# Decode attention over two caches on one core: PV in four column groups, V in one slot, 64 KB rows, B's heads in groups of eight

## The chip, the cores and the metric

The kernel runs on one core of a Trainium2 chip. A core has TensorE (PE: matrix multiplications into PSUM), VectorE (DVE), ScalarE (ACT), GpSimd (POOL) and SyncE (SP), each with its own in-order queue of instructions, and 16 DMA engines that move data between HBM and the on-chip memory SBUF (128 partitions). PE has a clock that a throttle grants in part. The metric is device microseconds from launch to end of the one core, the median of several runs.

## The reference

Two attention layers, A and B, each for one query token of 32 heads with 128 channels. A attends over all 16384 cached keys of each head, B over the last 4096. Then each multiplies by its output matrix, and the two rows of 512 are put side by side.

```python
def _A_ref(x, k_cache, v_cache, wq, wo):          # x [1,1,512], caches [1,32,16384,128] bf16
    q = ((x @ wq).reshape(B, Sq, 32, 128)).transpose(0, 2, 1, 3)
    scores = jnp.einsum("bhqd,bhkd->bhqk", q, k_cache) * (128 ** -0.5)
    p = softmax(scores, axis=-1)
    o = jnp.einsum("bhqk,bhkd->bhqd", p, v_cache)
    return o.transpose(0, 2, 1, 3).reshape(B, Sq, 32 * 128) @ wo
# _B_ref: the same over k_cache[:, :, Sk - W:], v_cache[:, :, Sk - W:], W = 4096
return jnp.concatenate([a, b], axis=-1)
```

The caches that are needed are A's K and V (134 MB each) and a quarter of B's (34 MB each); with the four matrices of 4 MB, 352 MB are read once.

## The kernel before

**Tiles.** The work is a sequence of 20 tiles T of 8 MB of K and 8 MB of V. Sixteen belong to A (two heads each: partition p holds 256 consecutive keys of one head, a row of 64 KB), four to B, at T = 0, 7, 13 and 19. A tile of B is two halves of 4 MB of four heads each: partition p holds 128 keys of head p mod 4, a row of 32 KB. K lives in a ring of two slots of 64 KB per partition (`kring`), V in a ring of two slots of 32 KB (`vring`), half a tile each, so that every V load is of 4 MB in rows of 32 KB.

**Scores, on VectorE.** For each half u of a tile, `scores_prod` (L206) multiplies K in place by the query, and `scores_tree` (L213, four additions that halve the width, and L219, a reduction) sums over the 128 channels. The scores land in `sc`.

**Softmax, per unit.** A unit is an A tile or half a B tile; there are 24. `unit_max` (L224, L226): the maximum per partition, turned into one row by a TensorE transpose. `max_all` (L231, L235, L238): the maximum per head, spread again over the partitions through PSUM. `soft` on ScalarE (L243, L246, L254): the bias, the exponential with its sum, and one copy of p per head, masked to that head's partitions, into `pm` (2 copies of 256 columns for A, 4 of 128 for B). `soft_sum` (L268, L273) and `recip` (L281, L283): the reciprocal of the head's sum.

**PV, on TensorE.** `pv` (L298): for each group of 4 keys per partition, one matmul with `pm` as weights (8 columns for A, 16 for B) and 512 columns of V as the moving operand, all summed in one PSUM tile `o` of 8 or 16 partitions, 32 matmuls per half. Row (h, c) of the result holds the right value in the c-th 128 of its 512 columns alone. `evict` (L314) scales it by the reciprocal on ScalarE, `columns` (L329, L333) picks the right parts and turns them to a column of `O` per head. In one A tile near the end (T = 17, `split`) the second half, and in the last B tile both halves, go through `pv_columns` instead (L344): 128 matmuls with V as the weights and 2 or 4 columns.

**End of a side.** `permute_o` (L365 to L374) reorders O, and the product with wo follows: for A in rows (L379, 32 matmuls), for B in columns by pieces of wo as they land (L393), then L399 to L406: add, transpose, cast, write out.

**Order.** The order on each engine is as written (no scheduler). All loads are issued by SP, in order, each waiting for its slot to be free: at the start wq of B, half of K(0), wq of A, the other half, K(1). Then at tile T: the first half of V(T-1), K(T+1), the second half of V(T-1); and the softmax and PV of tile T-1 run while VectorE makes the scores of tile T. K(T+1) needs VectorE to be done with K(T-1); a half of V needs the matmuls on the half before the last to be done. At the end come wo of A, both halves of V(19) and wo of B in five pieces. At the start `spread_x` and `project_q` (L183) make the queries on TensorE, with x in a K slot called `scratch` and wq in the V slots.

Of the kernel before, what the change touches and what calls it, by code (L numbers as in the profile page):

```python
# [25 lines left out]
def kernel(  # L26
# [26 lines left out]
    vring = ctx.enter_context(tc.tile_pool(name="vring", bufs=2))  # L53
# [4 lines left out]
    ps_o = ctx.enter_context(tc.tile_pool(name="ps_o", bufs=2, space=bass.MemoryType.PSUM))  # L58
# [5 lines left out]
    def vslot(name):  # L64
        return vring.tile([P, CH, DH], BF16, tag="vring", name=name)
# [9 lines left out]
    for s, n, x, wq, wo, nh in ((A, "A", A_x, A_wq, A_wo, 2), (B, "B", B_x, B_wq, B_wo, 4)):  # L75
        s.n, s.x, s.wq, s.wo, s.nh = n, x, wq, wo, nh
        s.xT = singles.tile([P, KC], BF16, tag=f"xT{n}", name=f"xT{n}")
        s.q = singles.tile([P, HQ // nh, DH], BF16, tag=f"q{n}", name=f"q{n}")
        s.O = singles.tile([P, HQ], BF16, tag=f"O{n}", name=f"O{n}")
        s.Op = singles.tile([P, HQ], BF16, tag=f"Op{n}", name=f"Op{n}")  # L80
        s.mask = singles.tile([P, nh], F32, tag=f"mask{n}", name=f"mask{n}")
        s.rows = singles.tile([P, nh, 4], F32, tag=f"rows{n}", name=f"rows{n}")
# [19 lines left out]
    def b_window(cache, g):  # L102
        return cache[0, 4 * g : 4 * g + 4, SkB - WB : SkB, :].rearrange("h (i l) d -> i h (l d)", l=CH)

    def a_pair(cache, g):
        return cache[0, 2 * g : 2 * g + 2, :, :].rearrange("h (i l) d -> (h i) l d", l=2 * CH)
# [4 lines left out]
    def load_k(T, u=None):  # L111
        s, g = steps[T]
        if s is A:
            nc.sync.dma_start(
                out=K[T][:, :, :].rearrange("p l d -> p (l d)"),
                in_=a_pair(A_k_cache, g).rearrange("p l d -> p (l d)"),
            )
        else:
            for v in (0, 1) if u is None else (u,):
                nc.sync.dma_start(  # L120
                    out=K[T][:, v * CH : (v + 1) * CH, :].rearrange("p l d -> p (l d)"),
                    in_=b_window(B_k_cache, 2 * g + v),
                )

    def load_v(T, u, dst=None):
        s, g = steps[T]
        V[T, u] = vslot("vt") if dst is None else dst
        if s is A:
            src = a_pair(A_v_cache, g)[:, u * CH : (u + 1) * CH, :].rearrange("p l d -> p (l d)")
        else:  # L130
            src = b_window(B_v_cache, 2 * g + u)
        nc.sync.dma_start(out=V[T, u][:, :, :].rearrange("p l d -> p (l d)"), in_=src)

    def load_wq(s):
        s.wq_t = vslot("wqt")
        nc.sync.dma_start(  # L136
            out=s.wq_t[:, :, :].rearrange("p a b -> p (a b)").rearrange("p (c f) -> p c f", c=KC),
            in_=s.wq.rearrange("(p c) f -> p c f", c=KC),
        )
# [9 lines left out]
    def make_masks(s):  # L149
        nc.vector.tensor_reduce(out=s.mask[:, :], in_=by_head(s, identf[:, :]), axis=AX.X, op=ALU.add)  # L150
        nc.vector.tensor_copy(s.rows[:, :, :], s.mask[:, :].unsqueeze(2).broadcast_to([P, s.nh, 4]))
# [22 lines left out]
    def project_q(s):  # L174
        wq = s.wq_t[:, :, :].rearrange("p a b -> p (a b)").rearrange(
# [13 lines left out]
    class Unit:  # L189
        def __init__(self, T, u):  # L190
            self.T = T
            self.s, g = steps[T]
            self.col = self.s.nh * g if self.s is A else self.s.nh * (2 * g + u)
            self.n = 2 * CH if self.s is A else CH
            self.rows = 4 * self.s.nh
            self.split = T == NT - 3
            self.last = self.split or T == NT - 1
            self.sc = one.tile([P, 2 * CH], F32, tag="sc", name="sc")

    units = {}  # L200

    def scores_prod(T, u):
        s, g = steps[T]
        k = K[T][:, u * CH : (u + 1) * CH, :]
        j = g if s is A else 2 * g + u
        nc.vector.tensor_tensor(out=k, in0=k, in1=s.q[:, j : j + 1, :].broadcast_to([P, CH, DH]), op=ALU.mult)  # L206

    def scores_tree(T, u):
        s, g = steps[T]
# [5 lines left out]
        if s is B or u == 0:  # L215
            units[T, u] = Unit(T, u)
        un = units[T, u if s is B else 0]
        c0 = u * CH if s is A else 0
        nc.vector.tensor_reduce(out=un.sc[:, c0 : c0 + CH], in_=k[:, :, 0:8], axis=AX.X, op=ALU.add)  # L219
        return un if s is B or u == 1 else None  # L220

    def unit_max(un):
        m = small.tile([P, 1], F32, tag="m", name="m")
        nc.vector.tensor_reduce(out=m[:, :], in_=un.sc[:, 0 : un.n], axis=AX.X, op=ALU.max)  # L224
# [3 lines left out]
    def max_all(un):  # L228
        s = un.s
        M = small.tile([1, 4], F32, tag="M", name="M")  # L230
# [3 lines left out]
        Mr = one.tile([1, P], F32, tag="Mr", name="Mr")  # L234
# [5 lines left out]
    def soft(un):  # L240
# [3 lines left out]
        p = one.tile([P, 2 * CH], BF16, tag="p", name="p")  # L244
        cs = small.tile([P, 1], F32, tag="cs", name="cs")
        nc.scalar.activation(  # L246
            out=p[:, 0 : un.n], in_=un.sc[:, 0 : un.n], func=ACT.Exp, scale=inv, bias=bias[:, :],
            accum_out=cs[:, :],
        )
        un.cs = cs  # L250
        pm = small.tile([P, 4 * CH], BF16, tag="pm", name="pm")
        un.pm = pm[:, 0 : un.n * s.nh].rearrange("p (i h c) -> p i h c", h=s.nh, c=4)
        for j in range(s.nh):
            nc.scalar.activation(  # L254
                out=un.pm[:, :, j, :], in_=p[:, 0 : un.n].rearrange("p (i c) -> p i c", c=4),
                func=ACT.Copy, scale=s.mask[:, j : j + 1],
            )

        if un.last:
            un.csm = small.tile([P, 4], F32, tag="csm", name="csm")  # L260
            nc.scalar.activation(
                out=un.csm[:, 0 : s.nh], in_=s.mask[:, :], func=ACT.Copy, scale=un.cs[:, :]
            )

    def soft_sum(un):
# [6 lines left out]
        else:  # L272
            nc.tensor.matmul(  # L273
                un.sm[0 : un.rows, 136:137], lhsT=s.rows[:, :, :].rearrange("p a b -> p (a b)"),
# [3 lines left out]
    def recip(un):  # L278
        un.r = small.tile([P, 4], F32, tag="r", name="r")
        if un.last:  # L280
            nc.vector.reciprocal(un.r[:, 0 : un.s.nh], un.sm[:, 136 : 136 + un.s.nh])  # L281
        else:
            nc.vector.reciprocal(un.r[0 : un.rows, 0:1], un.sm[0 : un.rows, 136:137])  # L283

    ready = []

    def pv(T, u):
        s = steps[T][0]
        un = units[T, u if s is B else 0]
        if un.split and u == 1:  # L290
            pv_columns(un, V[T, u], u * CH // 4)
            return
        first, final = (True, True) if s is B or un.split else (u == 0, u == 1)
        if first:
            un.o = ps_o.tile([16, 512], F32, tag="o", name="o")
        i0 = u * CH // 4 if s is A else 0
        for i in range(CH // 4):
            nc.tensor.matmul(  # L298
                un.o[0 : un.rows, :],
                lhsT=un.pm[:, i0 + i, :, :].rearrange("p a b -> p (a b)"),  # L300
                rhs=V[T, u][:, 4 * i : 4 * i + 4, :],
                start=(first and i == 0),
                stop=(final and i == CH // 4 - 1),
            )
        if final and not un.split:
            ready.append(un)

    evicted = []

    def evict():  # L310
        while ready:
            un = ready.pop(0)
            un.osb = one.tile([16, 512], F32, tag="o4", name="o4")
            nc.scalar.activation(  # L314
                out=un.osb[0 : un.rows, :], in_=un.o[0 : un.rows, :], func=ACT.Copy,
                scale=un.r[0 : un.rows, 0:1],
            )
            evicted.append(un)
            if ready:
                columns()  # L320

    def columns():
        while evicted:
            un = evicted.pop(0)
            s, n = un.s, un.rows
            oc = ps_s.tile([P, 4], F32, tag="sp", name="oc")
            sel = identf[0:n, 0:n].rearrange("k (h c) -> k c h", c=4)
            for j in range(4):
                nc.tensor.matmul(  # L329
                    oc[:, 0 : s.nh], lhsT=un.osb[0:n, j * P : (j + 1) * P], rhs=sel[:, j, :],  # L330
                    start=(j == 0), stop=(j == 3),
                )
            nc.scalar.copy(s.O[:, un.col : un.col + s.nh], oc[:, 0 : s.nh])  # L333

    def evict_part(un):
        un.part = one.tile([16, 512], F32, tag="o4", name="o4p")
        nc.scalar.copy(un.part[0 : un.rows, :], un.o[0 : un.rows, :])

    def pv_columns(un, V_t, i0):
        s, n = un.s, un.rows  # L340
        part = getattr(un, "part", None)
        o = ps_o.tile([P, 4], F32, tag="o", name="ocol")
        for l in range(CH):
            nc.tensor.matmul(  # L344
                o[:, 0 : s.nh], lhsT=V_t[:, l, :], rhs=un.pm[:, i0 + l // 4, :, l % 4],
                start=(l == 0), stop=(part is None and l == CH - 1),
            )
        if part is not None:
            sel = identf[0:n, 0:n].rearrange("k (h c) -> k c h", c=4)
            for j in range(4):  # L350
                nc.tensor.matmul(
# [178 lines left out]
```

## Time and profile before

| | |
|---|---|
| median of 3 runs | 827.59 us (827.15 to 827.60) |
| the profiled execution | 827.69 us, span from first to last instruction 825.8 us |
| VectorE busy | 761.7 us |
| TensorE busy (matmul) | 391.3 us |
| ScalarE busy | 67.1 us |
| loads on the DMA queue | 352.33 MB in 10376 packets |
| packets of 32 KB | 6528, mean 1220.2 ns |
| packets of 64 KB | 2048, mean 2425.7 ns |
| mean rate of the DMA | 427 GB/s |
| granted TensorE clock, mean | 0.702 |

How to read it: a line of a list of groups or of a timeline gives start, duration, engine, source line, operation and tiles (output <- inputs), and in brackets how long the engine sat idle before it and what ended that. The chain of waits is the chain of work that ended last, followed back from the end. A DMA packet is what one of the 16 engines moves in one piece: here, one row of one partition. A line of the table of windows gives a stretch in us, its length, and then what each engine did in it, the granted TensorE clock (1.00 is full), the share of the DMA engines and their rate.

### The profile page before, as it was taken

The numbers are of one execution on the slowest core, as the hardware profiler recorded it, in microseconds if no ns is written. First come the engines' busy times: TensorE is split into PE (matmuls) and PEld (weight loads), VectorE is DVE, ScalarE is ACT, GpSimd is POOL, SyncE is SP. The second block draws the span as 40 slices with busy tenths as digits, with TensorE's granted clock in tenths as the row PEclk, the third lists the DMA queues.
The fourth block names the chain that finished last, engine by engine and source line by source line (L and its number), as shares of the span: only waits on it lengthen the run. The fifth ranks groups of instructions, "written<-read, shape, count | busy, mean of one in ns | idle before, by whom it ended". The sixth has DMA issues, their size and how long they took to land.

```text
span 825.8 us, 5009 instructions
## 1 busy us (share of the span) xinstructions
PE 391.3 (47%) x2107; PEld 173.0 (21%) x2107; DVE 761.7 (92%) x361; ACT 67.1 (8%) x194; POOL 0.7 (0%) x6
## 2 busy tenths in 40 slices
PE   3505062808172644537180817354553617181794
PEld 1201020303031212212030302121221203030444
DVE  1899999999999999999999999999999999999930
ACT  0111010101000001101010100010010101010120
POOL 0000000000000000000000000000000000000000
PEclk9766576868585858677675859585767767575685
DMA  9999999999999999999999999999999999999996
GB/s 383 436 432 445 423 448 417 447 416 439 432 427 432 429 436 429 439 424 438 424 443 422 445 418 430 437 427 441 421 443 424 447 417 447 416 432 432 426 432 287
DMA packets 10404, 352.64 MB, mean 427 GB/s; under 512 B 1163, under 2 KB 1294, under 8 KB 1550
## 3 DMA queue, kind: packets, MB, share of 16 engines
q1 hardware_dynamic: 10376, 352.33, 99.2%
q8 instruction: 16, 0.26, 0.1%
q14 instruction: 6, 0.05, 0.0%
q10 hardware_dynamic: 6, 0.00, 0.0%
HBM read 352.32 MB, written 0.00 MB: 427 GB/s over the span
## 4 chain that ended last, share of the span: by engine, by line
DVE 77%; DMA 20%; PE 2%; issue 1%; SPq 0%; ACT 0%; DVEq 0%
DVE kt L206 35%; DVE kt L213 34%; DMA kt<-in_A_k_cache_dram 10%; DVE sc L219 5%; DMA kt<-in_B_k_cache_dram 5%; DMA wot<-in_B_wo_dram 4%; DMA vt<-in_A_v_cache_dram 2%; PE o L298 1%; DVE m L224 1%; DVE Mr L235 1%; DVE M L231 0%; PE ocol L344 0%; DVE r L283 0%; SPq L136 0%; SPq L146 0%
## 5 line engine op out<-in xcount | busy, mean ns | idle before, releaser
L213 DVE TENSOR_TENSOR kt<-kt 128x8192 bf16<-128x8192 bf16 (+3 forms) x160 | 344.9, 2156 | 4.7
L298 PE MATMUL o<-vt,pm 128*8 128x512 bf16 (+1 forms) x1184 | 300.1, 420 | 0.8 <-DMA vt<-in_A_v_cache_dram 0.8
L206 DVE TENSOR_TENSOR kt<-kt,qA 128x16384 bf16<-128x16384 bf16 x32 | 277.5, 8672 | 3.1 <-DMA kt<-in_A_k_cache_dram 3.0
L298 PEld LDWEIGHTS <-pm 128*8 128x8 bf16 (+1 forms) x1184 | 110.2, 94 | 181.5 <-issue 60.8
L226 PE MATMUL sm<-identf,m 128*1 128x128 f32 x24 | 8.5, 355 | 199.6 <-DVE m L224 199.5
L238 PE MATMUL sm<-one_f,Mr 1*128 1x1 f32 x48 | 13.1, 340 | 177.2 <-DVE Mr L235 177.2
L206 DVE TENSOR_TENSOR kt<-kt,qB 128x16384 bf16<-128x16384 bf16 x8 | 69.5, 8684 | 14.6 <-DMA kt<-in_B_k_cache_dram 14.6
L219 DVE TENSOR_REDUCE sc<-kt 128x128 f32<-128x1024 bf16 x40 | 48.8, 1220 | 3.3 <-DVE kt L213 0.5
L238 PEld LDWEIGHTS sm<-one_f,Mr 1*128 1x128 f32 x48 | 11.1, 285 | 184.1 <-DVE Mr L235 183.7
L226 PEld LDWEIGHTS sm<-identf,m 128*1 128x1 f32 x24 | 1.9, 79 | 202.2 <-issue 193.3
L243 ACT ACTIVATE bias<-sm 128x1 f32<-128x1 f32 x24 | 4.1, 171 | 404.0 <-PE sm L238 403.9
L314 ACT ACTIVATE o<-o,r 8x512 f32<-8x512 f32 (+1 forms) x21 | 14.3, 679 | 158.0 <-PE o L298 158.0
L329 PE MATMUL oc<-identf,o 8*128 8x2 f32 (+1 forms) x168 | 22.0, 249 | 2.9 <-ACT o L314 2.9
L329 PEld LDWEIGHTS oc<-identf,o 8*128 8x128 f32 (+1 forms) x168 | 20.2, 186 | 10.4 <-issue 6.5
L254 ACT ACTIVATE pm<-p,maskA 128x256 bf16<-128x256 bf16 x32 | 14.5, 500 | 0.5
L183 PE MATMUL qp<-wqt,xbA 128*128 128x512 bf16 x32 | 8.8, 444 | 9.5 <-DMA wqt<-in_A_wq_dram 9.5
L183 PE MATMUL qp<-wqt,scratch 128*128 128x512 bf16 x32 | 10.0, 488 | 5.3 <-DMA wqt<-in_B_wq_dram 5.3
L359 DVE TENSOR_TENSOR OB<-ocol,r 128x4 bf16<-128x4 f32 x2 | 0.3, 163 | 13.1 <-PE ocol L344 13.1
L246 ACT ACTIVATE p<-sc,bias 128x256 bf16<-128x256 f32 (+1 forms) x24 | 11.3, 472 | 0.8
L333 ACT CAST OA<-oc 128x2 bf16<-128x2 f32 x15 | 2.4, 161 | 102.6 <-PE oc L329 102.6
L254 ACT ACTIVATE pm<-p,maskB 128x128 bf16<-128x128 bf16 x32 | 10.2, 390 | 0.3
L224 DVE TENSOR_REDUCE m<-sc 128x1 f32<-128x256 f32 (+1 forms) x24 | 9.0, 374 | 0.6
(69 smaller groups left out, 98.6 us busy)
## 6 DMA issues: line engine op xcount, KB each, us to landing
vt<-in_A_v_cache_dram SPq DMA_DIRECT2D x32, 4096.0 KB, 26.5
kt<-in_B_k_cache_dram SPq DMA_DIRECT2D x8, 4096.0 KB, 35.3
vt<-in_B_v_cache_dram SPq DMA_DIRECT2D x7, 4096.0 KB, 33.2
wqt<-in_B_wq_dram SPq DMA_DIRECT2D x1, 4096.0 KB, 12.6
wqt<-in_A_wq_dram SPq DMA_DIRECT2D x1, 4096.0 KB
wot<-in_A_wo_dram SPq DMA_DIRECT2D x1, 4096.0 KB
wot<-in_B_v_cache_dram SPq DMA_DIRECT2D x1, 4096.0 KB, 29.3
wot<-in_B_wo_dram SPq DMA_DIRECT2D x1, 2048.0 KB, 26.9
```

The lines of the kernel that those rows point to most:

```text
L183: nc.tensor.matmul(qp[:, :, :], lhsT=s.xb[:, j, c, :], rhs=wq[:, c, j, g : g + 4, :], start=(k == 0), stop=(k == n - 1),)
L206: nc.vector.tensor_tensor(out=k, in0=k, in1=s.q[:, j : j + 1, :].broadcast_to([P, CH, DH]), op=ALU.mult)
L213: nc.vector.tensor_tensor(out=k[:, :, 0:w], in0=k[:, :, 0:w], in1=k[:, :, w : 2 * w], op=ALU.add)
L219: nc.vector.tensor_reduce(out=un.sc[:, c0 : c0 + CH], in_=k[:, :, 0:8], axis=AX.X, op=ALU.add)
L224: nc.vector.tensor_reduce(out=m[:, :], in_=un.sc[:, 0 : un.n], axis=AX.X, op=ALU.max)
L226: nc.tensor.transpose(un.sm[0:1, 0:P], m[:, :], identf[:, :])
L238: nc.tensor.matmul(un.sm[:, 128:129], lhsT=Mr[:, :], rhs=one_f[:, :], start=True, stop=True)
L246: nc.scalar.activation(out=p[:, 0 : un.n], in_=un.sc[:, 0 : un.n], func=ACT.Exp, scale=inv, bias=bias[:, :], accum_out=cs[:, :],)
L254: nc.scalar.activation(out=un.pm[:, :, j, :], in_=p[:, 0 : un.n].rearrange("p (i c) -> p i c", c=4), func=ACT.Copy, scale=s.mask[:, j : j ...
L298: nc.tensor.matmul(un.o[0 : un.rows, :], lhsT=un.pm[:, i0 + i, :, :].rearrange("p a b -> p (a b)"), rhs=V[T, u][:, 4 * i : 4 * i + 4, :], ...
L314: nc.scalar.activation(out=un.osb[0 : un.rows, :], in_=un.o[0 : un.rows, :], func=ACT.Copy, scale=un.r[0 : un.rows, 0:1],)
L329: nc.tensor.matmul(oc[:, 0 : s.nh], lhsT=un.osb[0:n, j * P : (j + 1) * P], rhs=sel[:, j, :], start=(j == 0), stop=(j == 3),)
```

## The change

- V is loaded a whole tile at a time, into one slot of 64 KB per partition, in rows of 64 KB. `load_v(T-1)` now stands alone ahead of K(T+1). Only the last tile's V comes in halves: the first into the free half of the K slot that holds wo of A, the second into the V slot with wo of B behind it.
- B takes eight heads to a tile (partition p holds 256 keys of head p mod 8), so that its K and V rows are of 64 KB too, and a tile of B is one softmax unit; there are 20 units instead of 24. K(0) is still loaded in halves.
- PV writes four regions of PSUM, partitions 0, 32, 64 and 96, in turn: 16 matmuls into each, 64 per tile in one burst. `oA` and `oB` are two fixed PSUM tiles of 128 partitions. `evict` reads all 128, `columns` multiplies by a `sel` matrix that adds the four regions up, `soft_sum` makes the sums on all 128 partitions, and A's unused rows are zeroed once.
- The split A tile is gone: only the last tile (B) goes through `pv_columns`, and there p is spread half on ScalarE, half on VectorE.
- B's queries are one group of eight heads (32 matmuls into one PSUM tile). Smaller tiles share slots (`Mr`, `oTs`, `rows` with `p`).
- At the tail, `permute_o(A)` and the product with wo of A stand ahead of the last unit's maximum on TensorE.

The program has 50 loads on SP instead of 72.

```diff
-    vring = ctx.enter_context(tc.tile_pool(name="vring", bufs=2))
+    vring = ctx.enter_context(tc.tile_pool(name="vring", bufs=1))
...
-        return vring.tile([P, CH, DH], BF16, tag="vring", name=name)
+        return vring.tile([P, 2 * CH, DH], BF16, tag="vring", name=name)
...
-    for s, n, x, wq, wo, nh in ((A, "A", A_x, A_wq, A_wo, 2), (B, "B", B_x, B_wq, B_wo, 4)):
+    for s, n, x, wq, wo, nh in ((A, "A", A_x, A_wq, A_wo, 2), (B, "B", B_x, B_wq, B_wo, 8)):
...
+        s.o = ps_o.tile([P, 512], F32, tag=f"o{n}", name=f"o{n}")
...
-    def load_v(T, u, dst=None):
+    def load_v(T):
         s, g = steps[T]
+        V[T] = vslot("vt")
+        nc.sync.dma_start(
+            out=V[T][:, :, :].rearrange("p l d -> p (l d)"),
+            in_=rows_of(s, A_v_cache if s is A else B_v_cache, g),
+        )
+
+    def load_v_half(T, u, dst):
+        s, g = steps[T]
+        V[T, u] = dst
+        nc.sync.dma_start(
+            out=dst.rearrange("p l d -> p (l d)"),
+            in_=rows_of(s, A_v_cache if s is A else B_v_cache, g)[..., u * CH * DH : (u + 1) * CH * DH],
+        )
...
+    def spread_p(un):
+        s = un.s
+        p = un.p[:, :].rearrange("p (i c) -> p i c", c=4)
         for j in range(s.nh):
             nc.scalar.activation(
+                out=un.pm[:, :, j, :], in_=p, func=ACT.Copy, scale=s.mask[:, j : j + 1]
+            )
...
+    def pv(un):
+        s, n = un.s, CH // 2
+        for i in range(n):
+            q = 32 * (i % 4)
+            nc.tensor.matmul(
+                s.o[q : q + un.rows, :],
+                lhsT=un.pm[:, i, :, :].rearrange("p a b -> p (a b)"),
+                rhs=V[un.T][:, 4 * i : 4 * i + 4, :],
+                start=(i < 4), stop=(i >= n - 4),
+            )
+
+    def evict(un):
+        un.osb = one.tile([P, 512], F32, tag="o4", name="o4")
+        nc.scalar.activation(out=un.osb[:, :], in_=un.s.o[:, :], func=ACT.Copy, scale=un.r[:, 0:1])
...
+        for T in range(NT):
+            if T >= 1:
+                load_v(T - 1)
                 if T + 1 < NT:
                     new_k(T + 1)
                     load_k(T + 1)
+            if T == NT - 1:
                 W = kslot("wot")
                 load_wo(A, W[:, 0:CH, :], (HQ,))
+                load_v_half(T, 0, W[:, CH : 2 * CH, :])
+            scores_prod(T, 0)
+            if T >= 1:
+                un = units[T - 1]
+                max_all(un)
+                soft(un)
+                spread_p(un)
+                soft_sum(un)
+                pv(un)
+            scores_tree(T, 0)
+            if T >= 1:
+                recip(un)
+                evict(un)
+                columns(un)
+            scores_prod(T, 1)
+            scores_tree(T, 1)
+            if T < NT - 1:
+                unit_max(units[T])
+        Z = vslot("wot")
+        load_v_half(NT - 1, 1, Z[:, 0:CH, :])
+        load_wo(B, Z[:, CH : 2 * CH, :], wo_pieces)
+        un = units[NT - 1]
         permute_o(A)
         project_out_rows(A)
+        unit_max(un)
+        max_all(un)
+        soft(un)
+        spread_p_half(un, 0, lambda o, i, m: nc.scalar.activation(out=o, in_=i, func=ACT.Copy, scale=m))
+        spread_p_half(un, 1, nc.vector.tensor_scalar_mul)
+        soft_sum(un)
+        recip(un)
         for u in (0, 1):
+            pv_columns(un, u)
+        scale_columns(un)
         permute_o(B)
         project_out_columns(B, wo_pieces)
```

## The prediction

> **What bounds the kernel now.** I read the page first: engines, queues, chain.
>
> ```profile
> span 825.8 us, 5009 instructions
> ...
> PE 391.3 (47%) x2107; PEld 173.0 (21%) x2107; DVE 761.7 (92%) x361; ACT 67.1 (8%) x194; POOL 0.7 (0%) x6
> ...
> DMA  9999999999999999999999999999999999999996
> ...
> q1 hardware_dynamic: 10376, 352.33, 99.2%
> ...
> DVE 77%; DMA 20%; PE 2%; issue 1%; SPq 0%; ACT 0%; DVEq 0%
> ```
>
> Two things look like bounds: VectorE (DVE) at 92%, which fills 77% of the chain of waits, and the DMA queue of SyncE (SP), whose packets fill 99.2% of 16 engines' span. The end of the chain of waits and VectorE's timeline at tile 16 decide between them.
>
> ```profile
> 595.64 1.23 DVE sc L219
> 596.89 39.91 DMA kt<-in_A_k_cache_dram
> 636.82 8.69 DVE kt L206
> ...
> 791.55 30.38 DMA wot<-in_B_wo_dram
> ```
>
> ```profile
> 598.01 8.69 DVE L206 TENSOR_TENSOR kt<-kt,qA 128x16384 bf16<-128x16384 bf16 x1 [0.70 <-DMA kt<-in_A_k_cache_dram]
> ```
>
> Until 590 us VectorE takes each A tile in 38.13 us (L206 starts at 81.13, 119.26, 157.40 in the chain) without waiting. From 598 on it waits for K. The packet records of the trace (size and duration of each) say why: a tile is 8 packets of 64 KB (K) plus 16 of 32 KB (V) on each of 16 engines. The engine that finishes first ends the first tiles' loads at 41.22, 60.58, 70.30, 80.0 us, so 19.36 us for an 8 MB K and 9.72 for a 4 MB half of V: 38.80 us a tile, 0.67 more than VectorE needs. An early lead of K over VectorE is eaten at that rate. The durations of all packets sum to 16 x 819.1 us, and data move from 2 to 821.8 us: no engine is ever idle. **The kernel is bound by its bytes**, then by 3.9 us from the last packet (L393's last matmuls, L399 to L406, the output's own DMA) to the end. Only fewer packets, or a shorter tail, can shorten it; VectorE's 92% is a near second bound.
>
> **The change part by part**
>
> Baseline: the profiled execution, 827.69 us, is a span of 825.8 plus 1.9 around it; the median of the runs shown is 827.59.
>
> *64 KB rows.* After 45 us a 32 KB packet takes 1218.7 ns (mean of 6016), a 64 KB packet 2425.8 (2016): two small ones cost 11.6 ns more than one large. All 32 halves of A's V, 6 of B's 8 K loads and 6 of its 8 V loads (4 MB each) become 64 KB rows: 44 x 128 = 5632 packets become 2816, 176 pairs on each engine, 176 x 11.6 ns = **2.0 us less**. Bounds: by the first engine's tile times (2 x 9.72 - 19.36 = 0.08 us, 22 tiles) 1.8; by the means with the slow first packets (2 x 1220.2 - 2425.7 = 14.6 ns) 2.6. The 22 fewer loads (72 to 50 on SP) save 22 semaphore writes of 9 ns per engine, 0.2, which the tile times hold already; I leave it out.
>
> *V in one slot.* Before, the next half of V waits for a half's matmuls; now V(T-1) waits until PV(T-2) has read all of V(T-2). SP is in order, so K(T+1), queued behind it, waits too. Cover: while PV(T-2) runs, K(T) is under way for 19.36 us. After V's last packet come about 0.5 us until TensorE (PE) sees it (L344's second run starts at 812.27, its load's last packet ends at 811.79), PV, and about 1.2 from issue to first packet (0.74 to about 1.8 at the start). So the engines run dry only if PV takes over 19.36 - 0.5 - 1.2 = **17.7 us**. K(T+1) itself needs VectorE to be done with K(T-1); K(T) has landed by then and VectorE runs at most 38.13 us per 38.7 us of DMA, so that comes some 18 us early.
>
> *PV over four column groups.* The same 64 matmuls a tile, with the output at partitions 0, 32, 64 and 96 in turn. Their present price:
>
> ```profile
> 148.95 15.71 PE L298 MATMUL o<-vt,pm 128*8 128x512 bf16 x64
> ```
>
> ```profile
> 148.00:152.00 4.00, 3.05 (x8) 0.98 (x9) 0.50 1.12 483
> 152.00:156.00 4.00, 4.00 (x19) 1.54 (x18) 0.94 1.16 496
> ```
>
> The second view is L298 by 4 us windows: PE busy, weight loads, granted clock, DMA. At clock 0.50 the pitch is 427 ns (weight loads 149.33, 149.76, 150.19 in the timeline), near full clock about 210. No two PV matmuls overlap in this trace (all go to one group), so four at a time is bounded by 15.71 us (no overlap) and 15.71/4 = 3.9 (perfect). I take 16 rounds at the cold pitch, **6.8 us**, because the clock rises only some 3.5 us into the burst. All of 3.9 to 15.71 is below 17.7: steady state pays nothing. It would be a loss only if the clock stayed at 0.50 without overlap (64 x 0.427 = 27.3).
>
> [...]
>
> *VectorE and ScalarE (ACT).* 24 softmax units become 20: four times m, M, Mr and r (283 + 272 + 233 + 146 ns), 3.7 us less on VectorE, worth nothing, as DMA paces it. B's spread of p becomes 8 x 500 ns = 4.0 us instead of 4 x 390; P is then ready some 14 us after K lands, while V lands 19 us after it. The eviction reads 128 partitions instead of 8 or 16; 8x512 and 16x512 both took 0.68 us, so I keep it. At the start, spread_x(B), sel and the memset of A.o add about 3 us to VectorE before 13.4 us, where TensorE waits for wq anyway (it waited 5.4). B's q is now one group of 32 matmuls: ready at 24.1 us (23.48 + 0.59) where L206 started at 23.13. The 1 us goes into the waits for K(0)'s second half (42.51) and, with one unit's m, M and Mr gone, K(1) (61.97). V(0) waits for both wq: 41.7 us; it is needed at 60.6.
>
> *The order of loads.* The whole V(0) now stands ahead of K(2), which lands about 10 us later (some 101 instead of 92), so VectorE is in step with DMA from tile 2 on and starts tile 19 near 762 us instead of 753.18. That eats cover in the tail.
>
> *Tail.* Its loads stand as before: wo of A, V(19) in halves, wo of B. VectorE ends tile 19 at 762 + 37.7 = 799.7. PV(18): V(18) in at 781.3, done at 788.1, evict and columns to 790.3, permute to 792, then L379's 32 matmuls (8.75 in this trace, cold start included) to 800.8. Behind them in TensorE's order waits the transpose of tile 19's maximum, wanted at 800.1. The maximum chain to the exponent's end as at 791.63 to 793.93 (about 2.4), csm 0.3, 8 spreads at 0.32: 806. V(19)'s halves take 3.6 us each; the second lands near 810.3, done at 813.9; the permutation ends at 815.3. The last piece of wo lands near 819.8, and its matmuls (4.2 us in all) wait for it as now. Slack is about 0.7 us, price 0; bounds 0 and 4.2 (L379 wholly at the cold pitch, 32 x 0.427 = 13.7 us, is 4.9 longer, less the slack). It is nearer to 0: L379 here follows a burst as closely as it will then.
>
> **Sum:** 825.8 - 2.0 + 0 + 0 = 823.8 span, plus 1.9: 825.7; from the median 827.59 - 2.0 = **825.6 us**. Its own range is 824.5 to 827: the 1.8 to 2.6 of the packets, the tail, and about 0.8 us either way because the engines drift apart (the last of them trails the first by 0.8 us at 42 us and by 3.9 at 714; fetches of instructions, 16 KB in about 1.05 us on one engine, fall differently).
>
> **Rivals**
>
> 1. *The groups do not overlap: slower.* PV stays at 15.7 us. Steady state still fits, but in the tail everything from PV(18) on comes 8.9 us later: L379 ends at 808 (its clock is then warm), p is spread at 813.5, the second half of V(19) is done at 820.7, the permutation at 822.2, wo's 4.2 us of matmuls at 826.6, plus 3.2: span 829.8, **831.7 us**. It decides from a PV of about 8.3 us. For it: no overlap is seen in this trace, and all four groups read the same 128 partitions of V. Against it: the output regions and weights are disjoint.
>
> 2. *Weight loads come out from under the matmuls.* 64 x 94 ns (L298's weight loads) = 6.0, PV 21.7 us, 4.0 over the cover, in 18 steps 72 us, and the tail 14 more: about **912 us**. Against it: within the burst the loads of 130 ns lie inside a pitch of 427 and the pitch does not show them. [...]
>
> 3. *The saving does not arrive.* Instruction fetches or part of the tail's 0 to 4.2 us eat it: **827.3**. For it: 2.0 us is the size of the engines' drift. Against it: the sum over all packets is steady.
>
> **How the numbers follow.** Forecast 0.66, rival 1 0.14, rival 2 0.05, rival 3 0.15. A difference under 0.2% (1.65 us) can't be told from none here; the forecast is 2.0. Of its 0.66, 0.48 lies below 825.93 and 0.18 above. Faster 0.48; same 0.18 + 0.13 = 0.31; slower 0.14 + 0.05 + 0.02 = 0.21. The range 824.0 to 830.0 holds the forecast and rival 3 and leaves out 0.19.
>
> **What would show it.** Right: K and V packets all of 64 KB at about 2425 ns; durations summing to about 817 us per engine; bursts of L302 of 4 to 9 us; VectorE waiting about 0.6 us for K before every tile from 2 on; the last wo piece landing near 820. Wrong: gaps in DMA where SP waits for PV; L302 bursts of 15 us or more; the last wo piece waiting for the permutation.

## The result, and the profile after

The changed kernel takes 1011.38 us (median of 6 runs, 1002.99 to 1043.87) against 827.27 us before (6 runs, 827.13 to 827.60): **1.2204 times as long, 95% interval 1.2139 to 1.2268** (the ratio leaves out the one run of 1043.87 us, which lies over 1.5% above the fastest). The prediction was 825.6 us. What follows reads the profiled execution, 1007.77 us with a span of 1005.9.

The page of the kernel after: span, the 40 slices of VectorE and of the DMA engines with their rate, the queue of the loads, the chain of waits.

```profile
span 1005.9 us, 4720 instructions
...
DVE  2659829999999468956999995599559999963920
...
DMA  9999999999999999999999999999999999999996
GB/s 292 292 334 250 248 418 441 433 422 449 420 438 344 207 349 397 208 302 417 446 427 433 438 357 207 341 409 208 290 438 427 431 435 431 370 211 297 338 222 204
...
q1 hardware_dynamic: 7208, 352.33, 99.2%
...
DVE 57%; DMA 21%; another core or an unknown queue 16%; issue 3%; PE 1%; ACT 0%; DVEq 0%; SPq 0%
```

The bytes are the same (352.33 MB), and the DMA engines are as full as before (99.2%). But the third row of slices falls from some 430 GB/s to 207 in places, while the row above it stays at 9. So the DMA engines do not stand idle for want of a free slot: **they are busy all the time, at half the rate, in some stretches**. VectorE idles in these slices or just behind them. Whom it waits for stands in the groups (busy time, mean of one in ns, then the idle time before them and its releaser).

```profile
L217 DVE TENSOR_TENSOR kt<-kt,qA 128x16384 bf16<-128x16384 bf16 x32 | 277.8, 8683 | 75.9 <-DMA kt<-in_A_k_cache_dram 75.8
L217 DVE TENSOR_TENSOR kt<-kt,qB 128x16384 bf16<-128x16384 bf16 x8 | 69.5, 8686 | 109.4 <-DMA kt<-in_B_k_cache_dram 109.4
```

The product itself costs what it cost before (8.68 us). B has 8 of the 40 products and over half of the waiting. One such wait in VectorE's timeline (start, duration; idle time in brackets), around the second tile of B, beside an A tile before it:

```profile
299.23 8.69 DVE L217 TENSOR_TENSOR kt<-kt,qA 128x16384 bf16<-128x16384 bf16 x1 [0.41 <-DMA kt<-in_A_k_cache_dram]
...
361.30 8.69 DVE L217 TENSOR_TENSOR kt<-kt,qB 128x16384 bf16<-128x16384 bf16 x1 [23.77 <-DMA kt<-in_B_k_cache_dram]
```

The A tile waits 0.41 us, about what the prediction said (0.6); the B tile 23.77. Of the 75.8 us of A, 71.5 are in the tiles just behind a tile of B. The view by windows, for a stretch in which only A loads and for one in which B's K lands (start:end, length, then PE, PEld, DVE, ACT, POOL busy with counts, granted clock, DMA share, GB/s):

```profile
130.00:300.00 170.00, 34.46 (x333) 16.98 (x325) 151.93 (x65) 10.95 (x30) 0.00 (x0) 0.58 1.00 434
315.00:355.00 40.00, 6.50 (x73) 2.79 (x72) 22.15 (x12) 0.85 (x2) 0.00 (x0) 0.59 1.02 212
```

The packet records say how. A's 64 KB packets take 2.42 us, as before. B's take 5.1 us, and B's 32 KB packets (the halves of the first K and the last V) 2.5 instead of 1.22. In all, 842 packets of 64 KB (mean 4984 ns) and 537 of 32 KB (mean 2425 ns) are slow: 72.8 MB, which is B's 67.1 MB and some packets of A beside them. They take 343.7 us of each engine where 842 x 2.421 + 537 x 1.216 over 16 engines would be 168.2: 175.5 us too much. All packets sum to 16 x 997.4 us against 819.1 before, +178.3; the span grew by 180.1. **Nearly the whole loss is the price of B's packets**, with those of A that run beside them.

And the part of the change that looked daring does what it should: PV's burst is 5.49 us where it was 15.71, in TensorE's timeline:

```profile
279.89 5.49 PE L302 MATMUL oA<-vt,pm 128*8 128x512 bf16 x64 [8.06 <-DMA vt<-in_A_v_cache_dram]
```

### The profile page after: what moved, and what is told of

Read it like the earlier page. It is cut to its first block, busy times and chain, and to the rows that moved or that the text cites. A ratio compares the mean times of both kernels' runs of the same rounds, so it can differ in the third digit from the quotient of the medians.

```text
span 1005.9 us, 4720 instructions
## 1 busy us (share of the span) xinstructions
PE 197.3 (20%) x1967; PEld 100.1 (10%) x1967; DVE 764.5 (76%) x358; ACT 64.3 (6%) x174; POOL 0.7 (0%) x6
## 3 DMA queue, kind: packets, MB, share of 16 engines
q1 hardware_dynamic: 7208, 352.33, 99.2%
## 4 chain that ended last, share of the span: by engine, by line
DVE 57%; DMA 21%; another core or an unknown queue 16%; issue 3%; PE 1%; ACT 0%; DVEq 0%; SPq 0%
DVE kt L217 27%; DVE kt L223 26%; DMA kt<-in_A_k_cache_dram 16%; DVE sc L228 4%; DMA kt<-in_B_k_cache_dram 3%; DMA wot<-in_B_v_cache_dram 2%; PE oA L302 1%; DVE m L235 0%; PE out_cols L370 0%; DVE Mr L246 0%; DVE M L242 0%; DVE r L296 0%; ACT p L257 0%; PE sm L249 0%
## 5 line engine op out<-in xcount | busy, mean ns | idle before, releaser
L217 DVE TENSOR_TENSOR kt<-kt,qA 128x16384 bf16<-128x16384 bf16 x32 | 277.8, 8683 | 75.9 <-DMA kt<-in_A_k_cache_dram 75.8
L302 PE MATMUL oA<-vt,pm 128*8 128x512 bf16 x1024 | 89.8, 527 | 138.3 <-DMA vt<-in_A_v_cache_dram 138.3
L302 PEld LDWEIGHTS <-pm 128*8 128x8 bf16 (+1 forms) x1216 | 38.8, 114 | 286.8 <-issue 262.0
L302 PE MATMUL oB<-vt,pm 128*32 128x512 bf16 x192 | 17.8, 552 | 87.6 <-DMA vt<-in_B_v_cache_dram 87.6
L311 ACT ACTIVATE o<-oA,r 128x512 f32<-128x512 f32 x16 | 11.0, 687 | 224.2 <-PE oA L302 224.2
L318 PE MATMUL oc<-selA,o 128*128 128x2 f32 x128 | 16.9, 254 | 12.7 <-ACT o L311 12.7
L318 PEld LDWEIGHTS oc<-selA,o 128*128 128x128 f32 x128 | 15.5, 191 | 20.8 <-ACT o L311 20.8
L288 PE MATMUL sm<-cs,rowsA 128*128 128x1 f32 x32 | 9.4, 362 | 14.5 <-ACT p L257 14.5
L329 PE MATMUL ocol<-pm,wot 128*128 128x8 bf16 x256 | 7.1, 168 | 21.2 <-DMA wot<-in_B_v_cache_dram 21.2
L257 ACT ACTIVATE p<-sc,bias 128x256 bf16<-128x256 f32 x20 | 10.2, 508 | 0.8 <-ACT bias L254 0.2
```

Source lines behind the costliest of these rows:

```text
L217: nc.vector.tensor_tensor(out=k, in0=k, in1=s.q[:, g : g + 1, :].broadcast_to([P, CH, DH]), op=ALU.mult)
L257: nc.scalar.activation(out=un.p[:, :], in_=un.sc[:, :], func=ACT.Exp, scale=inv, bias=bias[:, :], accum_out=un.cs[:, :])
L288: nc.tensor.matmul(un.sm[:, 136:137], lhsT=s.rows[:, :, :, :].rearrange("p r a b -> p (r a b)"), rhs=un.cs[:, :], start=True, stop=True,)
L302: nc.tensor.matmul(s.o[q : q + un.rows, :], lhsT=un.pm[:, i, :, :].rearrange("p a b -> p (a b)"), rhs=V[un.T][:, 4 * i : 4 * i + 4, :], st ...
L311: nc.scalar.activation(out=un.osb[:, :], in_=un.s.o[:, :], func=ACT.Copy, scale=un.r[:, 0:1])
L318: nc.tensor.matmul(oc[:, 0 : s.nh], lhsT=un.osb[:, j * P : (j + 1) * P], rhs=sel[:, j, :], start=(j == 0), stop=(j == 3),)
```

## The experiments

What differs between a load of A and one of B is not the packet's size but the form of the request. A's 128 rows are one run of HBM. B's tile has partition p = 8 i + h, so its request has 16 outer blocks (i) of 8 rows (h), the 8 heads 4 MB apart. Before, it was 32 blocks of 4. The first question is which of the two, addresses or blocks, makes a packet dear.

### Loads alone, by distance of the heads

Kernel `probe1` only loads, into a ring of three slots, each form twice; the edit is the body:

```diff
+    rows = ka[0].rearrange("h (r l) d -> (h r) (l d)", l=256)
+    def pitched(H, r0=0, heads=8):
+        v = rows[0 : (NR // H) * H, :].rearrange("(h r) f -> r h f", r=H)
+        return v[r0 : r0 + P // heads, 0:heads, :]
...
+        for rep in range(2):
+            load("pair", rows[0:128, :])
+            load("h4", pitched(64, 0, 4))
+            load("p1m", pitched(16))
...
+            load("p4m5", pitched(68))
+            load("hi", ka[0, 0:8, 0:4096, :].rearrange("h (r l) d -> h r (l d)", l=256))
```

> The kernel only loads and computes nothing (zeros are written out): twelve ways to fill a tile of 128 rows of 64 KB, twice over, each load queued behind the last. Names: pair (128 consecutive rows, as A's K), h4 (4 heads 4 MB apart, p = 4 i + h), p1m, p2m, p4m, p8m, p16m (8 blocks of 16 rows, blocks 1, 2, 4, 8, 16 MB apart, p = 8 i + h; p4m is what the changed kernel does for B, on A's cache), p4m4 and p4m5 (blocks 4 MB + 128 KB and 4 MB + 256 KB apart), hi (the same 8 heads, p = 16 h + i), after8 (B's cache as the changed kernel loads it), two64 (heads 0 to 3 and 4 to 7 as two loads of 64 rows). Theory 1, engines that read at the same moment at the same offset in heads 16 MB apart get in each other's way: p4m, after8 at about 5.1 us a packet and 40 us a load; p8m and p16m (32 and 64 MB) as slow; pair, h4, p1m, p4m4, p4m5 at 2.42 us and 19.4 us. Theory 2, eight interleaved blocks are slow whatever their distance: all p.. loads at 40 us, pair and h4 at 19.4. Theory 3, it is B's cache or the three-level form of the source: after8 slow and p4m fast, or h4 slow too.

Measured, for 8 MB each, from the packet records in order of start (first repetition):

```
form                                                 us per load   median packet, ns
pair: one run of 128 rows                            20            2418
h4: 32 blocks of 4 rows, 4 MB apart                  20            2418
p1m to p16m: 16 blocks of 8, 1, 2, 4, 8, 16 MB apart 41.1 to 41.6  5106 to 5109
p4m4, p4m5: the same, 4 MB + 128 KB, + 256 KB        41.6          5106, 5107
hi: 8 blocks of 16                                   80.6          10115
```

The distance of the heads plays no part: 1 MB and 4 MB plus 256 KB are as slow as 16 MB. Four interleaved heads cost nothing, eight double the price. With the head as the outer dimension (`hi`) the time doubles again, but its row is not clean: in this kernel the next load is queued behind, and some engines begin it while others are still at `hi`. The next experiment gives that form alone. For the same reason the loads behind `hi`, that is `after8`, `two64` and the second repetition, can't be told apart in the records and are left out; the packets that would by count be the second pair and h4 have medians of 3.7 and 5.1 us. The theory of an unlucky distance fell.

### Loads alone, by number of blocks

`probe2` loads one form at a time into one slot, all from nearly the same few megabytes of HBM, so that only the shape of the request differs:

```diff
+    def near(n, h):
+        return rows[0 : n * (h + 1), :].rearrange("(i h) f -> i h f", h=h + 1)[:, 0:h, :]
...
+        nc.sync.dma_start(out=slot("thirtytwo")[:, :], in_=near(32, 4))
+        nc.sync.dma_start(out=slot("sixteen")[:, :], in_=near(16, 8))
+        nc.sync.dma_start(out=slot("eight")[:, :], in_=near(8, 16))
+        nc.sync.dma_start(out=slot("four")[:, :], in_=near(4, 32))
+        nc.sync.dma_start(out=slot("lower")[0:64, :], in_=rows[0:64, :])
```

> Loads alone again (nothing is computed, zeros are written out), each alone on the DMA queue, all from the start of A's cache so that the addresses are nearly the same: flat (128 consecutive rows of 64 KB, one outer dimension of 128), spaced (every second row), and blocks of rows with one row left out between them, so that the source keeps two dimensions: sixtyfour (64 blocks of 2), thirtytwo (32 of 4, the form of B's loads before), sixteen (16 of 8, the changed kernel's form), eight (8 of 16), four (4 of 32); lower (64 consecutive rows into partitions 0 to 63), halves (two loads of 16 blocks of 4 into 64 partitions each, one behind the other), queues (the same two on two queues at once). Theory A, the number of blocks in the outer dimension decides, not the addresses: flat, spaced, sixtyfour, thirtytwo about 20 us; sixteen about 41, eight about 80, halves about 41 together. Theory B, the addresses (heads far apart) decide: all near 20 us except perhaps those into 64 partitions. If partitions 0 to 63 alone reach only half of the write paths, lower takes about 20 us for half the bytes, and queues comes out near 20 to 25.

SyncE's timeline of it (start and duration of each issue; each load waits for the one before, so the step to the next line is the load's time):

```profile
67.16 0.55 SPq L60 DMA_DIRECT2D thirtytwo<-in_A_k_cache_dram  x1
89.36 0.57 SPq L61 DMA_DIRECT2D sixteen<-in_A_k_cache_dram  x1
132.94 0.70 SPq L62 DMA_DIRECT2D eight<-in_A_k_cache_dram  x1
214.76 0.56 SPq L63 DMA_DIRECT2D four<-in_A_k_cache_dram  x1
375.41 0.53 SPq L64 DMA_DIRECT2D lower<-in_A_k_cache_dram  x1
```

32 blocks 22.2 us, 16 blocks 43.6, 8 blocks 81.8, 4 blocks 160.7, all for 8 MB from nearly the same place (one run of 128 rows 21.9, every second row 21.8, 64 blocks 22.7). The windows of the three slow ones (DVE and POOL busy, clock, DMA share, GB/s):

```profile
90.00:132.00 42.00, 0.00 (x0) 0.00 (x0) 1.00 0.96 200
134.00:214.00 80.00, 0.00 (x0) 0.00 (x0) 1.00 0.49 105
216.00:374.00 158.00, 0.00 (x0) 0.00 (x0) 1.00 0.25 53
```

By the DMA share, 16 blocks keep the 16 engines busy (0.96), 8 blocks half of them (0.49), 4 blocks a quarter (0.25). And the packets of all three have nearly the same price: median 5120, 5064 and 5000 ns, each about twice the 2418 of the fast forms. So two things add up. The shares are those of one block to an engine; that is an estimate from the shares, since the records name no engine. And in each of these forms a packet takes twice as long.

Issuing in two halves, on one queue or on two, took 42.5 and 41.2 us; the gain that a second queue might have brought (20 to 25 us) did not come, and why is not shown. The 64 rows of `lower`, contiguous in HBM, took 23.0 us for half the bytes: slow without any blocks. That points at the partitions that are written.

### Before, with B's loads in halves of 64 partitions

`before_halves` puts the suspected price, and nothing else of the change, into the kernel before: each 4 MB load of B is issued as two, with 16 blocks of 4 into 64 partitions. It is not the changed kernel's own form (16 blocks of 8 into all 128), but another that came out as dear in `probe2` (`halves`, 42.5 us).

```diff
-                nc.sync.dma_start(
-                    out=K[T][:, v * CH : (v + 1) * CH, :].rearrange("p l d -> p (l d)"),
-                    in_=b_window(B_k_cache, 2 * g + v),
-                )
+                for z in (0, 1):
+                    nc.sync.dma_start(
+                        out=K[T][64 * z : 64 * z + 64, v * CH : (v + 1) * CH, :].rearrange("p l d -> p (l d)"),
+                        in_=b_window(B_k_cache, 2 * g + v)[16 * z : 16 * z + 16],
+                    )
```

> The kernel before, with each of B's 15 loads of K and V in halves (4 MB, 32 blocks of 4 rows of 32 KB; all 16 of them) issued as two loads of 16 blocks of 4 rows into 64 partitions each. Same bytes, same rows, same places, no other change. Theory A (the form of the request decides): B's 67 MB run at half rate, 67.1 MB / 430 GB/s = 156 us more, about 980 us. Theory B (eight heads or their addresses decide): unchanged, 827 to 829 us.

Measured: 1035.45 us (4 runs, 1015.85 to 1042.57) against 827.41; the fastest run lies 188 us above before, near after's own loss. Its packets sum to 16 x 997.6 us, after's to 16 x 997.4: a dear form of B's request alone, with PV, V's slots and the softmax as before, brings a loss of the same size. That it lies over the expected 980 is in part the packets (178 us more than before, where 156 were expected) and in part idle time: packets fill 96.3% of the span here and 99.2% in after. The profiled execution, 1037.69 us, is near the upper end of the runs, and where the idle time comes from was not separated.

### Which side is it: reading or writing?

`probe3` loads the same rows of HBM into different partitions, one load at a time:

```diff
+        nc.sync.dma_start(out=slot("lower")[0:64, :], in_=rows[0:64, :])
+        nc.sync.dma_start(out=slot("even")[0:128:2, :], in_=rows[0:64, :])
+        nc.sync.dma_start(out=slot("first")[0:32, :], in_=rows[0:32, :])
+        nc.sync.dma_start(out=slot("fourth")[0:128:4, :], in_=rows[0:32, :])
+        nc.sync.dma_start(out=slot("top")[0:16, :], in_=rows[0:16, :])
+        nc.sync.dma_start(out=slot("half")[0:64:4, :], in_=rows[0:16, :])
+        nc.sync.dma_start(out=slot("eighth")[0:128:8, :], in_=rows[0:16, :])
+        nc.sync.dma_start(out=slot("whole")[:, :], in_=rows[0:128, :].rearrange("(h i) f -> i h f", i=16))
+        nc.sync.dma_start(out=slot("wide")[:, :], in_=rows[0:128, :].rearrange("(h i) f -> i h f", i=32))
```

> Loads alone again, one at a time (zeros are written out). The source is the same run of consecutive rows of 64 KB in every pair; only the partitions written differ. lower and even: 64 rows into partitions 0 to 63, and into every second one. first and fourth: 32 rows into partitions 0 to 31, and into every fourth. top, half and eighth: 16 rows (one to an engine) into partitions 0 to 15, into 0 to 60 by fours, and into 0 to 120 by eights. whole and wide: 128 consecutive rows, all partitions, but partition 8 i + h gets row 16 h + i (16 blocks of 8 by request) and partition 4 i + h gets row 32 h + i (32 of 4). Theory W, engines that write at the same time into partitions behind one write path share it: even and fourth at 2.4 us a packet, lower and first at about 5, top at about 10, half and eighth at about 5, whole 5, wide 2.4. Theory R, the rate is set on the reading side by the order in which rows are fetched: lower = even, first = fourth, top = half = eighth, all at 2.4 us.

The list of DMA issues of it (the last number is us from issue to landing):

```profile
flat<-in_A_k_cache_dram SPq DMA_DIRECT2D x1, 22.0
...
lower<-in_A_k_cache_dram SPq DMA_DIRECT2D x1, 22.8
even<-in_A_k_cache_dram SPq DMA_DIRECT2D x1, 12.4
first<-in_A_k_cache_dram SPq DMA_DIRECT2D x1, 12.4
fourth<-in_A_k_cache_dram SPq DMA_DIRECT2D x1, 7.9
top<-in_A_k_cache_dram SPq DMA_DIRECT2D x1, 11.6
half<-in_A_k_cache_dram SPq DMA_DIRECT2D x1, 7.6
eighth<-in_A_k_cache_dram SPq DMA_DIRECT2D x1, 7.6
...
wide<-in_A_k_cache_dram SPq DMA_DIRECT2D x1, 22.5
```

`lower` and `even` read the same 64 rows. Into partitions 0 to 63 they take 22.8 us with packets of 5119 ns, into every second partition 12.4 us with packets of 2420. **It is the writing side.** The smaller loads agree: 32 rows take 12.4 us into partitions 0 to 31 (`first`) and 7.9 into every fourth (`fourth`); 16 rows take 11.6 us into 0 to 15 (`top`), 7.6 into 0 to 60 by fours (`half`) and 7.6 into 0 to 120 by eights (`eighth`). The packets agree roughly with theory W: 8.65 us in `top` (about 10 expected), 4.75 and 4.87 in `half` and `eighth`, 2.64 in `fourth` (2.4 expected).

An estimate from these times: take 2.42 us for a row and about 2.6 us around a load; then the nine loads listed fit within 0.9 us with the time of 8 rows one behind the other in `flat`, `wide` and `lower`, of 4 in `even`, `first` and `top`, and of 2 in `fourth`, `half` and `eighth`. That is as if 16 rows went at a time in `flat`, `wide`, `even` and `fourth`, 8 in `lower`, `first`, `half` and `eighth`, and 4 in `top`. Why these sets of partitions differ is not shown.

B's form, 16 blocks of 8, writes all 128 partitions, as `flat` and `wide` do, so the set of partitions alone does not make it slow, and no load here separates reading from writing for this form. The records name no engine and no partition of a packet, so the order in which its rows are written is not shown. Why its packets take 5.1 us, and those of 32 blocks of 4 take 2.42, stays open.

The form `whole`, 16 blocks of 8 read from one run of 8 MB, took 43.2 us (issue at 105.32, the next at 148.52), and `wide`, 32 blocks of 4 from the same run, 22.5.

### The change with B's request put right

`fix4` is the changed kernel with B in groups of four heads again: each K and V tile of B comes as two loads of 32 blocks of 4 rows of 32 KB, and V's go into the halves of the one slot. A keeps its 64 KB rows; PV of B takes two column groups for each half, and B's softmax works by halves; all else stays as changed.

```diff
-    for s, n, x, wq, wo, nh in ((A, "A", A_x, A_wq, A_wo, 2), (B, "B", B_x, B_wq, B_wo, 8)):
+    for s, n, x, wq, wo, nh in ((A, "A", A_x, A_wq, A_wo, 2), (B, "B", B_x, B_wq, B_wo, 4)):
...
-        src = cache[0, 8 * g : 8 * g + 8, SkB - WB : SkB, :]
-        return src.rearrange("h (i l) d -> i h (l d)", l=2 * CH)
+        return cache[0, 4 * g : 4 * g + 4, SkB - WB : SkB, :].rearrange("h (i l) d -> i h (l d)", l=CH)
...
+        for v in (0, 1):
+            nc.sync.dma_start(
+                out=V[T][:, v * CH : (v + 1) * CH, :].rearrange("p l d -> p (l d)"),
+                in_=b_window(B_v_cache, 2 * g + v),
+            )
...
-        for i in range(n):
-            q = 32 * (i % 4)
+        for k in range(n):
+            q = 32 * (k % 4)
+            i = k if s is A else (k % 4) // 2 * (n // 2) + k // 4 * 2 + k % 2
```

> The changed kernel (column groups, one V slot of a whole tile, A's V in 64 KB rows) with B's heads back in groups of four and B's K and V in loads of 32 blocks of 4 rows of 32 KB. Theory A: all of the loss goes, and what the prediction said of the rest holds: packets fall by 4096 small to 2048 large, 128 pairs per engine x 11.6 ns = 1.5 us less, about 826.1 us, PV bursts of 5.5 us. Rival: the column groups or the single V slot cost something that the slow loads hid: 829 us or more.

Measured: **826.14 us** (11 runs, 825.86 to 826.24) against 827.41 before (15 runs, 827.14 to 827.69), ratio 0.9984, interval 0.9975 to 0.9993. The loss is gone. The gain on before is small, 0.16%, but the two sets of runs do not touch. Its page (the groups' columns as above):

```profile
span 824.3 us, 4774 instructions
...
q1 hardware_dynamic: 8072, 352.33, 99.1%
...
L228 DVE TENSOR_TENSOR kt<-kt,qA 128x16384 bf16<-128x16384 bf16 x32 | 277.9, 8683 | 9.8 <-DMA kt<-in_A_k_cache_dram 9.8
```

VectorE's wait for A's K shrinks from 75.8 us in the changed kernel to 9.8, the engines are 99.1% full with packets of 1.22 and 2.42 us that sum to 16 x 817.0. Against before, 128 pairs of packets on each engine have become one each: 128 x 11.6 ns is 1.5 us. The packets' sum fell by 2.1 us, the profiled span by 1.5, the median by 1.3. So everything else in the change is free to within about 1 us, as the prediction had it. TensorE's timeline in the tail:

```profile
781.56 5.11 PE L337 MATMUL oA<-vt,pm 128*8 128x512 bf16 x64 [8.67 <-DMA vt<-in_A_v_cache_dram]
...
791.27 8.75 PE L391 MATMUL out_row<-wot,OpA 128*1 128x512 bf16 x32 [1.63 <-DMA wot<-in_A_wo_dram]
...
810.72 3.57 PE L364 MATMUL ocol<-pm,wot 128*128 128x4 bf16 x128 [2.58 <-DMA wot<-in_B_v_cache_dram]
...
820.42 0.58 PE L405 MATMUL out_cols<-OpB,wot 128*128 128x1 bf16 x16 [0.45 <-DMA wot<-in_B_wo_dram]
```

The brackets of the last two lines name a load each time: the tail still waits for bytes and not for the work that was moved into it.

### What the column groups are worth

`fix4_onegroup` is `fix4` with PV of A summed in one column group, B's in one for each half:

```diff
-            q = 32 * (k % 4)
-            i = k if s is A else (k % 4) // 2 * (n // 2) + k // 4 * 2 + k % 2
+            i, w = k, n // s.hu
+            q = 64 * (k // w)
...
-                start=(k < 4), stop=(k >= n - 4),
+                start=(k % w == 0), stop=(k % w == w - 1),
```

> fix4 with PV of A in one column group (and B's halves one after the other in two), so that no two matmuls run at once. By the prediction's reckoning PV takes 15.7 us, the single V slot still costs nothing in the steady state (cover 17.7 us), and only the tail pays, about 6 us: 832 us. Rival: the slot's cover is smaller than reckoned and every tile pays some us: 850 us or more.

Measured: 844.24 us (4 runs, 843.16 to 847.74), 1.0211 times the kernel before, interval 1.0191 to 1.0230: slower, by about 2%. Neither expectation met it, 832 too low, 850 or more too high. Two bursts in TensorE's timeline, then the queue on the page:

```profile
280.03 16.01 PE L337 MATMUL oA<-vt,pm 128*8 128x512 bf16 x64 [9.06 <-DMA vt<-in_A_v_cache_dram]
320.46 16.27 PE L337 MATMUL oA<-vt,pm 128*8 128x512 bf16 x64 [11.29 <-DMA vt<-in_A_v_cache_dram]
```

```profile
q1 hardware_dynamic: 8072, 352.33, 97.5%
```

Here the engines do run dry while V waits for its one slot. The second PV ends at 336.73 and the next V is issued at 336.76; in the packet records 16 engines have a packet under way at 336 us, 12 at 337, 6 at 338, 12 at 339 and 16 again at 340. SyncE waits about 16.3 us for these matmuls after their V has landed, V's first packet starts at 338.09, 1.3 us after the issue, and the ten engines that are done with K by 337.74 get theirs between 338.12 and 339.22, up to 2.5 us after it. That makes 17.6 to 18.8 us, against 19.36 of cover by K. On average that would just fit, but the engines are not in step (their last packets of K end between 336.76 and 339.55), and those that are done with K first stand idle.

That is not all of it. In the profiled execution (847.74 us, the slowest of the four) the span is 21.5 us longer than in `fix4`, in three parts. Up to the loads' last packet (833.6, in `fix4` 820.2) it is 13.4 us: 7.3 are dearer packets (they sum to 16 x 824.3 against 817.0, in the same stretches as the gaps; why is not shown), and the remaining 6.1 are the gaps. Behind the last packet it is 8.2 us, the tail, for which about 6 were expected. There the last matmuls wait no longer for wo, as they did in `fix4`, but for the permutation:

```profile
838.97 3.56 PE L405 MATMUL out_cols<-OpB,wot 128*128 128x1 bf16 x128 [0.27 <-ACT OpB L386]
```

So one slot for V is free only together with the column groups, and these are worth 844.24 - 826.14 = 18.1 us here, by the medians.

## Why the prediction was wrong

**The step that failed is "*64 KB rows*"**: "All 32 halves of A's V, 6 of B's 8 K loads and 6 of its 8 V loads (4 MB each) become 64 KB rows". It priced B's new packets by their size, at the 2425.8 ns of the packets in before. All of those belong to A, whose request is one run of 128 rows. B's request changed its form as well, from 32 blocks of 4 rows to 16 of 8, and there the packet takes 5.1 us. No row of before shows that form, and the step gave no bounds for it. The form was named in the change ("partition p holds 256 keys of head p mod 8"), but no rival and no side of the range took it up, so that 1011 us lay outside of every case. The size of the error is nearly all that one term: 175.5 us too much on B's packets and their neighbours where the sum had a gain of 0.5 (48 of the 176 pairs were B's), of 182 us between the prediction and the profiled execution.

With the packet prices of `probe1` the loss can be added up, as an estimate: B's packets, worth 64 of 64 KB on each engine, at 5.1 us in place of 2.42 are 64 x 2.68 = 172 us more, where 175.5 were measured. Loads of B's form alone would have given that price beforehand.

Point by point, with `fix4` for what could not be seen behind the loss:

- *A's 64 KB rows*: right. 1.5 us of span for 128 pairs at 11.6 ns.
- *V in one slot*: the result (costs nothing) was right, the cover of 17.7 us too generous. It set the engines' drift at nothing and gave all engines the 1.2 us from issue to first packet; at the place looked at the first of them had it (1.3), others only after up to 2.5. By `fix4_onegroup` the limit lies below 16.3 us; at 5 to 6 us it does not matter.
- *PV over four groups*: right in kind. 6.8 us was predicted, 4.9 to 6.4 measured for A's bursts, between the bounds of 3.9 and 15.71. Rival 1 (no overlap) and rival 2 (weight loads exposed) are out. Rival 1 also had the wrong price, 831.7 us where `fix4_onegroup` takes 844: its tail was near (8.2 us measured), but without overlap the steady state pays as well, where it had nothing.
- *The order of loads*: VectorE "waiting about 0.6 us for K before every tile from 2 on" agrees: 0.41 us in after's undisturbed A tiles, and 9.8 us over 16 A tiles in `fix4`.
- *Tail*: in `fix4` the product with wo of A ends at 800.0 (800.8 predicted), the second half of V(19) is done at 814.3 (813.9), the last piece of wo begins at 820.4 (near 819.8 landed). Price 0, as taken.
- *What would show it*: "durations summing to about 817 us per engine" was the test that decided: 997.4 in after, 817.0 in `fix4`. The view was well chosen, but the step behind it lacked one input, the form of the request.

With B's form kept, the kernel takes 826.14 us: the 825.6 of the prediction, plus 0.56 for B's 48 pairs, which that kernel leaves small, is 826.2. An agreement to 0.1 us is partly luck, since the median of before was 827.59 in the prediction and 827.41 in this comparison.

## What to carry to other kernels

A packet's price is not a matter of its size alone (64 KB took 2.42 us in A's form and 5.1 in B's): before a layout is changed to get longer rows, write down the request's outer dimension and the partitions it fills, and measure that form alone in a kernel that only loads, with nothing queued behind it. Busy DMA engines at half their rate look in a profile like full ones (here a share of 1.02 at 212 GB/s and of 1.00 at 434); it is the row of GB/s, and the durations of packets of one size, that tell contention from a bound by bytes. And when two edits cover for one another, as the column groups do for the single V slot, each has to be judged with the other in place.

## What the runs showed of the hardware

- With an outer dimension of 16 (64 KB rows, SyncE's queue), loads into 128 partitions run at 200 GB/s (`sixteen`) and 198 (`whole`); with 32 blocks at 400 (`wide`, by windows). At 8 and 4 blocks the DMA share falls too: 0.49 and 105 GB/s at 8, 0.25 and 53 at 4. Distances in HBM from 1 to 16 MB, padded or not, made no difference (41.1 to 41.6 us).
- Loads of 64 neighbouring partitions are as slow in us as loads of 128 (22.8 against 22.0), every second partition is not (12.4).
- 64 matmuls with 8 columns of weights, over four column groups, take 4.9 to 6.4 us (A's bursts in after), where one group takes 16.0 and 16.3 in the two bursts of `fix4_onegroup` above. In the burst of 5.49 us the weight loads come four at a time, about 427 ns apart at its start (280.27, 280.69, 281.12) and 216 later (284.13, 284.34), while the four matmuls before them still run by the profile (280.27 to 280.90).
- The runs of the two kernels with the slow form scatter by 27 and 41 us, those of `fix4` by 0.4. Why is not shown.
